# Where a batch's left-over queries stand in the slot order of a fused top-k attention and feed-forward kernel

## The chip, the cores and the metric

The kernel runs as one program on one core of one Trainium2 chip. The metric is the device time of one execution in microseconds; lower is better. Three runs of the kernel before gave 1451.66, 1452.44 and 1452.67 us, so the median is 1452.44 us.

## The reference

Attention with a top-k mask is followed by a two-layer network with a quick-GELU:

```python
# q, k, v: (8, 8, 576, 64); w_in: (512, 2048); w_out: (2048, 512); all float32
scores = (1 / sqrt(64)) * matmul(q, k.transpose(0, 1, 3, 2))        # 576 x 576 for each of 64 heads
kth    = np.partition(scores, -32, axis=-1)[..., -32:-31]            # the 32nd largest of each row
scores = where(scores >= kth, scores, -1e9)
attn   = exp(scores - max); attn = attn / (sum(attn) + 1e-9)
x      = matmul(attn, v).transpose(0, 2, 1, 3).reshape(4608, 512)    # tokens x (head, head_dim)
h      = x @ w_in
out    = (h * sigmoid(1.702 * h)) @ w_out                            # 4608 x 512
```

## The kernel before, in words

**Slots.** Each of the 8 batches has 8 heads, taken as 4 pairs, and 576 queries. 576 is four tiles of 128 queries and 64 left over. A slot is one piece of attention work: 128 query rows for two "heads" of 576 keys. A full slot is one tile of 128 queries for one pair of heads, `(b, t, (hp, hp))`, so there are 16 of them in a batch. The left-over 64 queries of two pairs share one slot, `(b, NF, (hp, hp + 1))`, so there are 2 more; the code calls these `ends`. That makes 18 slots in a batch (`PER`) and 144 in all. The list `slots` (lines 277 to 284) is their order.

**One slot through the engines.** `scores` (line 287) makes the products on TensorE (PE), line 297. `copy_scores` brings them to SBUF on ScalarE (ACT), line 309. `topk_of_pairs` (line 354) finds the 32nd largest on VectorE (DVE) with rounds of MAX8 and MATCH_REPLACE8 (lines 369 and 372); `pair_up` (line 333) makes the larger of each two scores on DVE, line 338, and the smaller on GpSimd (POOL), lines 342 and 352. `mask` and `exps` (lines 426 and 434) run on ACT, `invert` (lines 442 and 444) on DVE, `normalize` (line 457) on POOL. `split` (lines 489 to 495) takes the float32 words apart into halves on ACT and stores them in DRAM; `turn_by_dma` (line 501) brings them back transposed as the tile `pt`. `values_at` (line 560) multiplies `pt` with the values `v_l` and `v_e` on PE, and `x_of` (lines 574 and 577) copies the result into `xT` on ACT.

**Blocks.** `xT` has five places of 128 rows by 512 columns. Place `(b, t)` is complete when the four pairs of tile `t` are done; the ends of an even batch and of the odd batch after it share one place, which is complete when the odd batch's ends are done. `finish_x` then puts a `Block` on the list `ready`. A block is 16 column tiles of the hidden layer. `hidden` (line 605) makes one unit: with one block ready it takes 4 column tiles of this block, 16 matmuls with 128 moving columns; with two blocks ready it takes 2 column tiles of both together, 8 matmuls with 256 moving columns (line 621, many == 2). Either way a unit fills one PSUM bank, and a block is 4 units' worth. `tanh` (lines 643 and 646, ACT), `gate` (lines 655 and 656, POOL) and `project` (line 676, PE, 4 matmuls of 512 columns) take each unit further; `leave` (line 684) brings a finished block out.

**The order of work.** Everything is recorded in one order by hand (`manual_schedule`). Slots 0 to 10 go one by one (`slot`). From slot 11 on, `two_slots(n)` handles slots n and n + 1; it is called a step below. In a step PE gets, in this order: the first `hidden` unit and a `project`, the scores of slot n + 2, the values of slots n - 3 and n - 2 (`held`), the scores of slot n + 3, the second `hidden` unit, and a `project`. When `ready` is empty, `hidden` does nothing. After the last step `last_slot` works off what is left.

**The table of loads.** `later` maps a slot to calls. For batch b and pair hp, relative to the batch's first slot: `FETCH` says when q and k are loaded (q at the number, k one slot later), `READY` when they are split for the transposing load (`prepare_by_dma`, lines 248 to 261), and `VALUES` when `load_v` (lines 200 and 208, three DMAs) runs. All of these DMAs are issued by the queue of SyncE (SP), in program order, between `split`'s store (line 495) and the transposing load (line 501) of the same slot:

```python
        if live(n):
            split(n)
        begin(todo[1])          # loads of v, q and k that stand at slot n + 1
        if live(n):
            turn_by_dma(n)
```

Of the kernel before, what the change touches and what calls it, by code (L numbers as in the profile page):

```python
# [30 lines left out]
def kernel(  # L31
# [32 lines left out]
    NP = H // 2  # L64
# [212 lines left out]
    slots = []  # L277
    for b in range(B):

        full = [(b, t, (hp, hp)) for t in range(NF) for hp in range(NP)]  # L280
        ends = [(b, NF, (hp, hp + 1)) for hp in range(0, NP, 2)]
        slots += full[: -NP] + ends + full[-NP:]
    N = len(slots)
    PER = N // B
    st = [{} for _ in slots]
# [419 lines left out]
    def at(n, fn, *args):  # L705
        later.setdefault(n, []).append((fn, args))
# [1 line left out]

    READY = (-13, -9, -5, -1)
    READY_1 = (-5, -3, -1, 1)
    FETCH = (-17, -15, -11, -7)
    FETCH_1 = (-11, -9, -4, -2)
    VALUES = (0, 1, 2, 3)
    by_slot = dict(enumerate([2, 2, 3, 3, 3, 3, 3, 3, 3, 3, 3, 1]))
    for n in by_slot:
        first = sum(map(len, list(by_slot.values())[:n]))
# [10 lines left out]
    for b in range(1, B):  # L729
        for hp in range(NP):  # L730
            if b > 1:
                for i, name in enumerate("qk"):
                    at(b * PER + FETCH[hp] + i, load, name, b, hp)
                at(b * PER + READY[hp], prepare_by_dma, b, hp)
            else:
                at(b * PER + FETCH_1[hp], load_both, b, hp)
                at(b * PER + READY_1[hp], prepare_by_pe, b, hp)
            at(b * PER + VALUES[hp], load_v, b, hp)
    unfinished = []
    early = []  # L740
    finished = []
# [335 lines left out]
```

## Time and profile before

| What | Value |
|---|---|
| Median of the runs | 1452.44 us (1451.66 to 1452.67) |
| The profiled execution's own time | 1453.04 us |
| Its span in the trace | 1451.2 us |
| PE, PEld busy | 1414.1 us (97%), 995.2 us (69%) |
| DVE busy | 1361.8 us (94%) |
| ACT, POOL busy | 1159.9 us (80%), 985.2 us (68%) |
| Granted TensorE clock | 0.991 |
| DMA bytes moved | 244.40 MB, mean 168 GB/s |

PE is TensorE's matmuls and PEld its weight loads; DVE, ACT, POOL and SP are VectorE, ScalarE, GpSimd and SyncE, and SPq and its like are an engine's own queue, where DMAs are issued. A float32 matmul of the program is two records in the trace, so a unit of 16 matmuls shows as x32 and a unit of 8 as x16. A busy share is an average over stages: which engine sets the pace has to be read stage by stage. The span has three of them: up to about 240 us, where weights are prepared and the first slots run; 240 to 1366 us, where step follows step; and the tail after the last scores at 1366 us.

### The profile page before, as it was taken

To read this page: it belongs to the slowest core of one execution; us is meant where nothing else is said; L and a number is where in the kernel's file an instruction comes from. 1 tells how busy PE (TensorE), PEld (TensorE's weight loads), DVE (VectorE), ACT (ScalarE), POOL (GpSimd) and SP (SyncE) were. 2 spreads that over 40 slices of the span, in tenths; PEclk is the share of its full clock that TensorE was granted. 3 is DMA by queue.
4 is the path that set the end of the run, shared out by engine and by line. 5 is a ranking of instruction groups with operands and counts; after the bars stand their busy time and mean duration, and the time that the engine had idled before them with its cause. 6 is when DMAs were issued, how large, how long until landed. Compare 5 with 4: busy or idle time off the path is not lost.

```text
span 1451.2 us, 29107 instructions
## 1 busy us (share of the span) xinstructions
PE 1414.1 (97%) x9524; PEld 995.2 (69%) x9524; DVE 1361.8 (94%) x4703; ACT 1159.9 (80%) x1862; POOL 985.2 (68%) x1181
## 2 busy tenths in 40 slices
PE   7889899999999999999999999999999999999998
PEld 5667567777666667777666667777666667777665
DVE  7999999999999999999999999999999999999910
ACT  6998887888888887888888888888878888777730
POOL 4888766676766777766667677766777777667610
PEclk8999999999999999999999999999999999999999
DMA  7542467766777768778677767867677776544430
GB/s 212 162 160 63 139 164 195 184 180 171 190 199 186 176 172 209 188 177 189 167 190 185 186 176 185 209 177 186 163 199 192 183 177 179 163 134 129 137 90 15
DMA packets 521272, 244.40 MB, mean 168 GB/s; under 512 B 457376, under 2 KB 495264, under 8 KB 521120
## 3 DMA queue, kind: packets, MB, share of 16 engines
q1 hardware_dynamic: 520688, 242.25, 64.2%
q8 instruction: 75, 1.23, 0.3%
q14 instruction: 77, 0.63, 0.1%
q10 hardware_dynamic: 432, 0.30, 0.1%
HBM read 45.09 MB, written 103.42 MB: 102 GB/s over the span
## 4 chain that ended last, share of the span: by engine, by line
PE 85%; DVE 11%; ACT 1%; DMA 1%; SPq 1%; issue 1%; POOL 0%; DVEq 0%; POOLq 0%
PE ph L621 33%; PE po L676 31%; PE o L560 10%; PE s_ps L297 10%; DVE top L319 3%; DVE left L322 3%; DVE top L369 2%; DVE left L372 1%; DMA pt<-rows 1%; DVE greater L338 0%; ACT sc L493 0%; DVE lesser L372 0%; DVE wout L154 0%; POOL pr L457 0%; DVE win L154 0%
## 5 line engine op out<-in xcount | busy, mean ns | idle before, releaser
L621 PEld LDWEIGHTS ph<-xT,win 128*128 128x128 f32 x3520 | 484.3, 191 | 86.0 <-issue 54.5
L621 PE MATMUL ph<-xT,win 128*128 128x128 f32 (+1 forms) x3520 | 537.4, 309 | 1.0 <-ACT xT L542 0.6
L676 PE MATMUL po<-wout,th 128*128 128x512 f32 x1152 | 519.3, 593 | 4.9 <-POOL wout L149 3.9
L493 ACT COPY sc<-pr 128x2304 uint16<-128x2304 uint16 x134 | 283.1, 2113 | 163.6 <-POOL pr L457 163.6
L676 PEld LDWEIGHTS po<-wout,th 128*128 128x128 f32 x1152 | 213.0, 190 | 217.8 <-issue 205.1
L369 DVE MAX8 top<-left 128x8 f32<-128x288 f32 x810 | 328.0, 446 | 0.0
L342 POOL TENSOR_TENSOR lesser<-sc,greater 128x576 int32<-128x576 int32 x135 | 190.6, 1412 | 177.1 <-DVE greater L338 177.1
L457 POOL TENSOR_SCALAR pr<-pr,rden 128x576 f32<-128x576 f32 x268 | 196.4, 745 | 127.4 <-DVE top L376 76.8
L372 DVE MATCH_REPLACE8 left<-top,left 128x288 f32<-128x288 f32 x540 | 234.8, 442 | 0.0
L434 ACT ACTIVATE pr<-sc,low 128x576 f32<-128x576 f32 x288 | 220.8, 773 | 0.0
L369 DVE MAX8 top<-lesser 128x8 f32<-128x288 f32 x540 | 218.0, 444 | 0.0
L426 ACT ACTIVATE sc<-sc,cut 128x576 f32<-128x576 f32 x288 | 207.4, 774 | 1.8 <-POOL cut L413 1.7
L309 ACT ACTIVATE sc<-s_ps 128x576 f32<-128x576 f32 x288 | 171.0, 648 | 37.1 <-PE s_ps L297 36.2
L352 POOL TENSOR_TENSOR lesser<-lesser,sc 128x576 int32<-128x576 int32 x135 | 190.6, 1412 | 0.2
L297 PE MATMUL s_ps<-qk_t 64*128 64x288 f32 (+1 forms) x1280 | 182.7, 431 | 0.5 <-ACT qk_t L220 0.5
L656 POOL TENSOR_TENSOR th<-th,h 128x512 f32<-128x512 f32 x131 | 167.6, 1279 | 11.2 <-POOL th L655 0.4
L297 PEld LDWEIGHTS s_ps<-qk_t 64*128 64x128 f32 (+1 forms) x1280 | 99.3, 177 | 78.1 <-issue 60.1
L560 PE MATMUL o<-pt,v_l 128*64 128x128 f32 (+1 forms) x2400 | 145.9, 265 | 3.7 <-DMA pt<-rows 3.5
L560 PEld LDWEIGHTS o<-pt,v_l 128*64 128x64 f32 x2400 | 121.4, 137 | 31.3 <-issue 16.9
L338 DVE TENSOR_TENSOR greater<-sc 128x576 f32<-128x576 f32 x135 | 133.2, 986 | 0.0
L655 POOL TENSOR_SCALAR th<-th 128x512 f32<-128x512 f32 x131 | 80.9, 617 | 58.8 <-ACT th L643 58.8
L643 ACT ACTIVATE th<-ph 128x512 f32<-128x512 f32 x144 | 85.5, 594 | 40.1 <-PE ph L621 35.5
(78 smaller groups left out, 1355.5 us busy)
## 6 DMA issues: line engine op xcount, KB each, us to landing
rows<-sc SPq DMA_DIRECT2D x134, 576.0 KB, 3.2
qk_rows<-halves SPq DMA_DIRECT2D x48, 256.0 KB, 2.8
qk_l<-in_q_dram SPq DMA_DIRECT2D x64, 128.0 KB, 3.4
raw<-in_moe_w_in_dram SPq DMA_DIRECT2D x16, 512.0 KB, 4.6
v_l<-in_v_dram SPq DMA_DIRECT2D x32, 256.0 KB, 3.7
raw<-in_moe_w_out_dram SPq DMA_DIRECT2D x16, 512.0 KB, 3.5
out_dram<-ob SPq DMA_DIRECT2D x32, 256.0 KB, 2.9
qk_l<-in_k_dram SPq DMA_DIRECT2D x62, 128.0 KB, 3.4
```

Of the source, the lines that this page charges most:

```text
L297: nc.tensor.matmul(ps[i][rows, c, 0:HALF], lhsT=qT[b, hps[p]][on, cols], rhs=kT[b, hps[p]][on, FIRST[i] + c * HALF : FIRST[i] + (c + 1) * ...
L342: nc.gpsimd.tensor_tensor(out=whole, in0=a.bitcast(I32), in1=greater[n][:].bitcast(I32), op=ALU.subtract)
L352: nc.gpsimd.tensor_tensor(out=whole, in0=whole, in1=b.bitcast(I32), op=ALU.add)
L369: nc.vector.max(found(r, i, True), src[:, i, :])
L372: nc.vector.match_replace(to[:, i, :], found(r, i), src[:, i, :], LOWEST)
L426: nc.scalar.activation(sc[:, i, :], sc[:, i, :], AF.Prelu, bias=cut[:, i : i + 1], alpha=HUGE)
L434: nc.scalar.activation(pr[:, i * S : (i + 1) * S], sc[:, i, :], AF.Exp, bias=low[:, i : i + 1], accum_out=den[:, i : i + 1],)
L457: nc.gpsimd.tensor_scalar(pr[:, i, :], pr[:, i, :], st[n]["rden"][:, i : i + 1], 1.0, op0=ALU.mult, op1=ALU.mult)
L493: nc.scalar.copy(out=halves, in_=pr[:].bitcast(U16).rearrange("p (k h) -> p h k", h=2))
L560: nc.tensor.matmul(o[j * D : (j + 1) * D, cols], lhsT=main[:, j, c, :] if c < NF else tail[:, j, :], rhs=pt[:, MAIN[j] + c if c < NF else ...
L621: nc.tensor.matmul(ph[:, i * many * P : (i + 1) * many * P], lhsT=win[:, c, f * P : (f + 1) * P], rhs=xs[:, first : first + step * (many - ...
L676: nc.tensor.matmul(x.po[:], lhsT=gT[:, i * P : (i + 1) * P], rhs=wout[:, f, :], start=(x.done == 0), stop=(x.done == FC - 1))
```

## The change

In even batches the two `ends` slots move from positions 12 and 13 of the batch to 16 and 17, the last. In odd batches they move to positions 4 and 5, behind the first four full slots. The full slots keep their order among each other. In odd batches the third pair's q and k are split two slots later, and the loads of v stand at slots 2, 2, 3 and 4 of the batch instead of 0, 1, 2 and 3. (`READY` is used from the third batch on; the second batch has `READY_1`, which is not changed.)

```diff
-        slots += full[: -NP] + ends + full[-NP:]
+        first = NP if b % 2 else len(full)
+        slots += full[:first] + ends + full[first:]
...
-    READY = (-13, -9, -5, -1)
+    READY = (-13, -9, -5, -1), (-13, -9, -3, -1)
     READY_1 = (-5, -3, -1, 1)
     FETCH = (-17, -15, -11, -7)
     FETCH_1 = (-11, -9, -4, -2)
-    VALUES = (0, 1, 2, 3)
+    VALUES = (0, 1, 2, 3), (2, 2, 3, 4)
...
-                at(b * PER + READY[hp], prepare_by_dma, b, hp)
+                at(b * PER + READY[b % 2][hp], prepare_by_dma, b, hp)
...
-            at(b * PER + VALUES[hp], load_v, b, hp)
+            at(b * PER + VALUES[b % 2][hp], load_v, b, hp)
```

No instruction on SBUF data is added or removed in attention. What changes with the slot order is when blocks become ready. Before, a batch pair's nine blocks are complete at slots 3, 7, 11, 17, 21, 25, 29, 31 and 35 of its 36; after, at 3, 7, 11, 15, 21, 23, 27, 31 and 35. Of the 144 units of `hidden`, the program before makes 68 with two blocks and 76 with one; the changed program makes 112 with two and 32 with one.

## The prediction

> **What bounds the kernel now.** I read the chain of waits first. It is almost all PE:
>
> ```profile
> PE 85%; DVE 11%; ACT 1%; DMA 1%; SPq 1%; issue 1%; POOL 0%; DVEq 0%; POOLq 0%
> ```
>
> In order of time the DVE part lies before 240 us. From there to 1366 us the chain is PE without a gap, in two kinds of step, one after the other here:
>
> ```profile
> 1200.09 3.65 PE ph L621 x16
> 1203.74 3.43 PE po L676 x8
> 1207.17 3.45 PE ph L621 x16
> 1210.63 3.43 PE po L676 x8
> ...
> 1218.74 3.77 PE ph L621 x32
> 1222.51 3.44 PE po L676 x8
> 1225.94 3.57 PE ph L621 x32
> 1229.51 3.44 PE po L676 x8
> ...
> 1237.62 3.77 PE ph L621 x32
> ```
>
> A step with two-block (wide) units lasts 18.65 us (1200.09 to 1218.74), one with one-block (single) units 18.885 us. From the step whose values start at 258.74 to the one at 1366.17 there are 29 single and 30 wide steps: 29 x 18.885 + 30 x 18.65 = 1107.2, against 1107.4 in the trace.
>
> PE's lead is thin, though. In a wide stage the timeline of DVE shows the line of `pair_up` at a fixed spacing:
>
> ```profile
> 401.92 1.26 DVE L338 TENSOR_TENSOR greater<-sc 128x576 f32<-128x576 f32 x1
> ...
> 411.60 0.73 DVE L338 TENSOR_TENSOR greater<-sc 128x576 f32<-128x576 f32 x1
> ...
> 420.61 1.25 DVE L338 TENSOR_TENSOR greater<-sc 128x576 f32<-128x576 f32 x1
> ```
>
> 9.68 + 9.01 = 18.69 us, in every wide step. DVE has no gap there, so this is its own floor, 0.04 above PE's wide step. In single stages it is held up; the view of line 442 from 250 to 1366 us says by whom:
>
> ```profile
>   ACT pr L434: 3.0, 11
> ```
>
> ACT waits for PE and DVE for ACT, 3.0 us in all. Summed over the L338 spacings, DVE loses 4.2 us to PE over the 117 slots after 251 us. A PE saving beyond that meets DVE.
>
> The third thing is SP's queue. Between a slot's store (L495) and its transposing load (L501) stand the loads of that slot. Slot 2 of a batch is the fullest now (timeline of SP):
>
> ```profile
> 400.02 0.35 SPq L495 DMA_DIRECT2D rows<-sc  x1
> 400.43 0.43 SPq L200 DMA_DIRECT2D v_l<-in_v_dram  x1
> 400.90 1.62 SPq L208 DMA_DIRECT2D v_e<-in_v_dram  x2
> 402.57 1.27 SPq L186 DMA_DIRECT2D qk_l<-in_k_dram  x2
> 403.89 0.63 SPq L189 DMA_DIRECT2D qk_l<-in_k_dram  x1
> 404.63 2.49 SPq L501 DMA_TRANSPOSE pt<-rows  x1
> ```
>
> Load L501 comes 4.6 us after the store; without loads it is 2.85. It lands 4.5 to 4.8 us after its issue here, and the values that need it (second half of L560) start at 410.32, 5.7 after it. So 1.1 us are to spare, in the wide stage, where PE is never idle.
>
> **Part 1, wider units.** The changed program has 44 more wide units in place of single ones: 22 steps x 0.235 us = 5.2 us less on PE. The row behind it is 3.77 against 3.65 and 3.57 against 3.45: 0.12 us for each unit.
>
> The Trainium skill (TensorE: Matmul & The Clock Gate, section "Wait — 56ns, not 53.3ns?") gives a fixed cost of about 2.5 ns for a matmul on a warm array. By it the 16 fewer records of a wide unit would save 0.04 us, 1.8 us in all, where the rows give 0.12 and 5.2. The measured rows decide.
>
> **Part 2, DVE's floor.** DVE's work is the same. 59 steps at 18.69 are 1102.7 us against 1106.9 now, so DVE alone gives back at most 4.2 us.
>
> The Trainium skill (Perfetto Trace Analysis, section "Identifying the Most-Contended Engine") judges TensorE by its weight loads and the other engines by occupancy. That reads 69% against DVE's 94% and makes DVE the bound; the sum by it would be DVE's own waits, 3 to 4 us, not 5.2. The chain's row names PE. Here both are nearly bounds.
>
> **Part 3, the start.** Two `hidden` calls find no block ready. Now they are the second of step 17 and the first of step 19 (203 to 216 us), in the changed order the second of 21 and the first of 23. So PE has 14.3 us more to do just when it is still catching up. I follow it from the scores that end at 207.69: single unit, project, split of q and k, unit, project give the scores of slot 21 at 223.0 (now 216.6); values of ends, scores, unit, project end at 234.8, and `leave` of the third block waits for that on ACT (now 231.8). DVE's L442 waits for the exponentials behind it: about 3.45 us later, at 238.3, now 235.6. So DVE is 2.7 us late; 0.5 of this is the L338 that runs 1.25 instead of 0.74 beside a gate, given back in the step without one. The store that is at 249.64 now comes at 252.35, effectively 251.85 after that 0.5. PE then has a step with little to do and waits; its values start at 259.1 (now 258.74). Bounds: 0 late if ACT had slack there, 4 if the wait recurs; I take 2.2 net, as the L684 row at 231.78 has only 0.3 us of slack to L442.
>
> **Part 4, the loads of v.** In odd batches slot 2 now carries two `load_v` and k of the next batch: nine issues ahead of L501. The extra three cost 0.43 + 1.62 and gaps, 2.1 us. L501 is then issued 4.6 + 2.1 = 6.7 us after its store; plus 4.6 to land, minus 1.15 (the first half of L560 comes first), values may start 10.15 us after the store ("the need"; 6.7 us usually). Now that distance is 9.4 at its largest in a single stage, 8.9 in a wide one. Queued behind L501 on SP is only the next store; waiting for it is PE, and PE is in order, so scores, units and projects wait too. Batches 1, 3 and 5 have this; in batch 1 PE waits for DVE anyway, and in batch 7 there is no next k (need 8.2, covered). Need from both sides: 8.05 if the extra issues hide like today's, 12.5 if an issue is held 1 us (the L189 at 572.03 took 1.59, not 0.63) and the landing takes 6. I take 10.15, since every duration has its row.
>
> **Part 5, the rest at nothing.** The third split moves from step -5 to -3: one ACT copy (L248, 2.1 us), four issues on SP (2.3 us) and one transposing load (3.3 us). Step -3 has no loads in the changed order, ACT is 80% busy, and the keys are needed a step later; uncovered it costs 2.1 us in each of three batches. The other v loads move away from slots 0 and 1 (lighter by 2.1) to slot 4 (k and v, 4.6, need 8.05). Ends cost PE the same in any place, and at least two xT places stay free.
>
> **The sum,** by starts of values. To batch 3: DVE stores at 251.85 + 17 x 18.69 = 569.6; + 10.15 = 579.7, now 577.55. PE alone would be there at 259.1 + 18.89 + 16 x 18.65 = 576.4, so it stalls 3.3 us. To batch 5: 569.6 + 18 x 18.69 = 906.0, plus 1.2 because PE, now late, holds DVE until the distance is back near 9.0; + 10.15 = 917.3, now 915.24; PE alone 915.9. To the last step, 24 steps: 4 x 18.885 + 20 x 18.65 = 448.5 against 450.9: 1365.8 against 1366.17. The tail of 85 us has the same units (8 wide, 2 single). So 0.4 us less than the profiled 1453.04; off the median of 1452.44 that is 1452.0. The end moves by twice the need: 1345.5 + 2 x need.
>
> **Rivals.** A: the need is hidden (under 8.9). Then the slot-4 loads of batch 5 set PE's date: 924.7 + 8.05, and 3 single and 20 wide steps follow: 1362.4, so 1448.6 us. For it: 1.1 us to spare now; against it: the queue is in order and 2.1 exceeds 1.1. B, slower: the nine issues in a row are held up and the landing is late. At a need of 12.2 the end is 1369.9, 1456.1 us; it decides from a need of 11.8. For it: the 1.59 above and landings up to 6.8 in the trace; against it: L501 on the second slot mostly lands in 4.5 to 4.8. C: DVE's floor gives way because POOL's gate no longer overlaps L338 (it does so by 0.64 in every step now), 18.18 a step. Then PE alone counts, 5.1 us less: 1447.3. Against it: the overlap is the same at distances from 8.9 to 9.6.
>
> **How the numbers follow.** Forecast (need 9 to 11.8, 1449.5 to 1455.3): 0.62. A: 0.19. C: 0.05. B: 0.14. No change is within 0.2% (2.9 us), about what a measurement of this kernel tells apart. So faster 0.24, same 0.62, slower 0.14. The range, 1448.4 to 1455.6, takes in A and the start's bounds and leaves out C and most of B.
>
> **What would show it.** Right: x1792 records of L621 with 256 columns; L338 spaced 18.69 across long wide stages; PE waiting for pt<-rows near 578 and 916 us, 1 to 3.5 us each; L501 6.7 us behind its store there. Wrong: no such waits (A), more than 4 us of them (B), L338 spacing under 18.6 (C), or DVE waits of many us elsewhere.

## The result and the profile after

| | Before | After |
|---|---|---|
| Median of the runs | 1452.44 us (1451.66 to 1452.93, 5 runs) | 1457.77 us (1457.22 to 1460.18, 5 runs) |
| Profiled execution, its span | 1453.04, 1451.2 us | 1457.92, 1455.8 us |
| Granted TensorE clock | 0.991 | 0.987 |
| PE, DVE busy | 1414.1, 1361.8 us | 1411.8, 1361.6 us |

The changed kernel is slower: the ratio is 1.0040, with an interval of 1.0025 to 1.0055. The forecast was 1452.0 us and the range ended at 1455.6. Neither engine has more to do; PE even has 2.3 us less. In the changed kernel the helpers' lines stand one further down (L339 for L338, L443 for L442, L496 and L502 for the store and the turning load, L561 for the values, L622 and L677 for the units).

The chain of waits by engine of the kernel after is cut short, since it can be followed back only to 822 us:

```profile
PE 36%; DVE 6%; SPq 0%; DMA 0%; ACT 0%; issue 0%; POOL 0%; ACTq 0%
```

What it covers is PE again. In order of time, the place that was shown of before now has wide units throughout, and a step takes 18.65 us (1206.49 to 1225.14):

```profile
1206.49 3.65 PE ph L622 x16
1210.14 3.43 PE po L677 x8
1213.58 3.45 PE ph L622 x16
1217.03 3.43 PE po L677 x8
...
1225.14 3.65 PE ph L622 x16
```

So this stage is as forecast. The slot that was to decide, the second of batch 3, is as forecast too (timeline of SP; start, duration):

```profile
574.21 0.35 SPq L496 DMA_DIRECT2D rows<-sc  x1
...
576.73 0.59 SPq L200 DMA_DIRECT2D v_l<-in_v_dram  x1
...
578.52 1.27 SPq L186 DMA_DIRECT2D qk_l<-in_k_dram  x2
...
580.56 2.67 SPq L502 DMA_TRANSPOSE pt<-rows  x1
```

The turning load is issued 6.35 us after the store (forecast 6.7) and lands at 585.24, and PE waits for it (timeline of PE; in brackets the idle time and what ended it):

```profile
585.38 1.09 PE L561 MATMUL o<-pt,v_l 128*64 128x128 f32 x16 [1.17 <-DMA pt<-rows]
```

The loss is elsewhere. The best measure of it is the start of each slot's store, which follows DVE, against the same slot's store in before. The table has it for the kernel after and for five of the experiments below, in us behind before (slots count from 0). At slot 10, where the slot orders don't differ yet, the other profiles lie from 0.1 us ahead of before to 0.8 us behind it (fetch_shifted, which has products added ahead of that slot, lies 2.9 behind), so differences of this size say nothing:

| Slot (before at) | after | start_only | batch0_k_earlier | v_late_only | both_mended | all_but_batch0 |
|---|---|---|---|---|---|---|
| 12 (165.4) | 0.66 | -0.07 | -0.17 | -0.12 | 0.04 | 0.37 |
| 13 (175.2) | 2.42 | 1.56 | 1.51 | -0.12 | 1.85 | 0.37 |
| 17 (212.8) | 2.70 | 1.84 | 2.12 | -0.32 | 2.13 | -0.32 |
| 18 (221.1) | 4.62 | 3.76 | 4.03 | -0.32 | 2.13 | -0.32 |
| 20 (239.8) | 5.56 | 5.55 | 5.00 | 0.89 | 2.14 | -0.31 |
| 22 (258.5) | 6.23 | 5.92 | 6.18 | 2.37 | 3.21 | -0.33 |
| 25 (287.1) | 6.73 | 6.04 | 6.17 | 2.82 | 2.17 | -0.31 |
| 55 (568.2) | 6.02 | 5.42 | 6.26 | 3.06 | 2.32 | -0.74 |
| 61 (624.8) | 6.75 | 5.23 | 6.24 | 4.60 | 2.24 | -1.27 |
| 97 (962.5) | 7.35 | 5.23 | 6.24 | 5.44 | 1.92 | -2.37 |
| 143 (1391.7) | 5.01 | 5.23 | 6.24 | 5.44 | -0.21 | -4.37 |

The kernel after is 6.7 us late by slot 25. Behind it the column stays between 6.0 and 7.4 us and ends at 5.0. The windows of the start tell how. First before, then after (columns: window, its length, busy time and instructions of PE, PEld, DVE, ACT and POOL, granted clock, DMA share, GB/s):

```profile
165.00:170.00 5.00, 5.00 (x52) 4.34 (x49) 5.00 (x20) 4.61 (x10) 2.94 (x4) 1.00 0.32 126
200.00:240.00 40.00, 38.11 (x253) 24.50 (x251) 39.66 (x145) 31.93 (x54) 25.62 (x33) 1.00 0.69 173
258.00:264.00 6.00, 6.00 (x71) 4.91 (x68) 6.00 (x22) 5.59 (x12) 3.42 (x4) 1.00 0.68 161
264.00:270.00 6.00, 6.00 (x33) 4.09 (x32) 5.93 (x25) 3.75 (x5) 4.21 (x7) 1.00 1.06 223
```

```profile
165.00:170.00 5.00, 3.31 (x28) 2.55 (x32) 5.00 (x17) 3.19 (x5) 2.96 (x4) 0.67 0.33 128
200.00:240.00 40.00, 40.00 (x341) 29.44 (x341) 37.65 (x133) 32.21 (x58) 26.55 (x33) 1.00 0.58 153
258.00:264.00 6.00, 1.25 (x21) 1.01 (x20) 5.90 (x25) 4.68 (x5) 4.63 (x6) 0.86 0.88 213
264.00:270.00 6.00, 5.56 (x36) 4.22 (x37) 5.93 (x23) 4.03 (x10) 1.68 (x2) 0.57 0.53 183
```

There are three things to see. From 200 to 240 us the roles of PE and DVE are exchanged: PE is busy without a gap and DVE loses 2 us, where before DVE was full and PE had 1.9 us to spare. From 258 to 264 us PE has next to nothing to do. And at 165 and at 264 us the clock falls to 0.67 and 0.57, where before it is 1.00. The two falls go with the two longest waits of PE for a turned block:

```profile
166.69 1.97 PE L561 MATMUL o<-pt,v_l 128*64 128x128 f32 x16 [2.24 <-DMA pt<-rows]
...
264.44 1.97 PE L561 MATMUL o<-pt,v_l 128*64 128x128 f32 x16 [5.19 <-DMA pt<-rows]
```

The same 16 records take 1.09 us after the wait of 1.17 us above, and 1.97 here. The second wait is in the step with little to do. Its block belongs to slot 21, and in the changed order this slot's loads hold a v as well as k, so the turning load is issued 4.57 us after the store (timeline of SP), where before it was 3.30:

```profile
255.19 0.35 SPq L496 DMA_DIRECT2D rows<-sc  x1
...
259.76 2.33 SPq L502 DMA_TRANSPOSE pt<-rows  x1
```

### The profile page after: what moved, and what is told of

It is laid out like the page before. It is cut to its first block, busy times and chain, and to the rows that moved or that the text cites. A ratio compares the mean times of both kernels' runs of the same rounds, so it can differ in the third digit from the quotient of the medians.

```text
span 1455.8 us, 27733 instructions
## 1 busy us (share of the span) xinstructions
PE 1411.8 (97%) x8820; PEld 973.2 (67%) x8820; DVE 1361.6 (94%) x4703; ACT 1159.2 (80%) x1862; POOL 984.7 (68%) x1181
## 5 line engine op out<-in xcount | busy, mean ns | idle before, releaser
L622 PE MATMUL ph<-xT,win 128*128 128x256 f32 (+1 forms) x2816 | 532.3, 344 | 0.5 <-ACT xT L543 0.5
L677 PE MATMUL po<-wout,th 128*128 128x512 f32 x1152 | 519.1, 593 | 4.9 <-POOL wout L149 3.9
L622 PEld LDWEIGHTS ph<-xT,win 128*128 128x128 f32 x2816 | 453.9, 191 | 101.3 <-issue 48.5
L677 PEld LDWEIGHTS po<-wout,th 128*128 128x128 f32 x1152 | 216.4, 190 | 220.5 <-issue 205.1
L561 PE MATMUL o<-pt,v_l 128*64 128x128 f32 (+1 forms) x2400 | 147.8, 267 | 10.3 <-DMA pt<-rows 10.2
L561 PEld LDWEIGHTS o<-pt,v_l 128*64 128x64 f32 x2400 | 122.5, 138 | 38.9 <-issue 25.5
L339 DVE TENSOR_TENSOR greater<-sc 128x576 f32<-128x576 f32 x135 | 133.0, 985 | 1.9 <-ACT sc L310 1.9
```

What stands on the lines that cost most here:

```text
L561: nc.tensor.matmul(o[j * D : (j + 1) * D, cols], lhsT=main[:, j, c, :] if c < NF else tail[:, j, :], rhs=pt[:, MAIN[j] + c if c < NF else ...
L622: nc.tensor.matmul(ph[:, i * many * P : (i + 1) * many * P], lhsT=win[:, c, f * P : (f + 1) * P], rhs=xs[:, first : first + step * (many - ...
L677: nc.tensor.matmul(x.po[:], lhsT=gT[:, i * P : (i + 1) * P], rhs=wout[:, f, :], start=(x.done == 0), stop=(x.done == FC - 1))
```

## The experiments

Each kernel was timed beside the kernel before on the same chip. Ratios are to that kernel, with their intervals; its medians were 1452.4 to 1453.1 us.

### Is it the start?

**from_batch2**: the new order and the late loads of v from batch 2 on only.

```diff
-        first = NP if b % 2 else len(full)
+        first = (NP if b % 2 else len(full)) if b > 1 else len(full) - NP
-            at(b * PER + VALUES[b % 2][hp], load_v, b, hp)
+            at(b * PER + VALUES[b % 2 if b > 1 else 0][hp], load_v, b, hp)
```

> The new slot order and the later loads of v hold from the third batch on; the first two batches are as before. Theory S (the loss is made in the start: PE gets two more units between 200 and 240 us, runs dry afterwards and comes back on a lower clock): the store that the profile of before has at 249.6 us is back there, and with 104 wide units and the two fuller load slots (batches 3 and 5, one wait of up to 1 us and one of 1 to 2 us) the time is about 1450.7 us. Theory L (the loss is made later, by the waits for the values' transposing loads and the new places of the left-over slots): about 1457 us, as the changed kernel's 1457.8.

Measured: 1453.45 us, 1.0002 (0.9993 to 1.0011). The loss is gone, but there is no gain. The time lies between what the two theories gave. Behind the start its PE waits 4.3 us for turned blocks, 1.4 of it behind the nine issues of batch 3 and 2.7 behind those of batch 5, more than in the kernel after (2.5 us).

**start_only**: the other half, batches 0 and 1 changed and the rest as before.

```diff
+        first = (NP if b % 2 else len(full)) if b < 2 else len(full) - NP
+                at(b * PER + READY[0][hp], prepare_by_dma, b, hp)
+            at(b * PER + VALUES[b == 1][hp], load_v, b, hp)
```

> The kernel after with the new places of the left-over slots (and the late loads of v) in batches 0 and 1 alone; the order, the split of q and k and the loads of v of batches 2 to 5 as before. Theory P (the step in which TensorE has few or no units of the output stage moved back from steps 17 to 19, where its slack let TensorE catch up, to steps 21 to 23, where TensorE is late already; five steps of 19.9 us then hold VectorE, which needs 18.7): the start loses by itself what it lost in the kernel after, 4.9 to 6 us, and nothing later gives it back, so about 1458.0 us. Rival R (the start's lag is there only because of what the later order takes away, or is taken back by VectorE's own pace later): 1455.0 or less.

Measured: 1459.04 us, 1.0045 (1.0032 to 1.0057). The start alone loses 6.2 us, and little gives it back: the table's column is 6.0 at slot 25 and 5.2 from slot 61 to the end. Theory P holds in that the start loses this much by itself; R is out.

### Mending one thing in the kernel after

**units_postponed**: the two units that replaced empty calls in steps 17 and 19 are skipped, so they are made later, when PE has little to do.

```diff
-        hidden(ps_t if opens else None)
+        if n != 19:
+            hidden(ps_t if opens else None)
...
-        hidden(ps_t)
+        if n != 17:
+            hidden(ps_t)
```

> The changed kernel with its slot order and loads whole, but the second unit of step 17 and the first of step 19 are left for the two calls of steps 21 and 23 that found no block. So PE has in each step of the start what it has before the change. Theory S: no run-dry wait of 5 us near 260 us, store of slot 21 near 250 us instead of 255.2, time about 1450 us. Rival (the left-over slots at 16, 17, 22 and 23 cost the start by themselves, not the units' dates): 1456 us or more.

Measured: 1458.41 us, 1.0032 (1.0020 to 1.0045). The wait of 5 us near 260 us is gone in its profile, as Theory S had it, and the store of slot 21 is 2.5 us behind before and not 5.6. But PE now waits for the block behind the nine issues of batch 1, and the clock falls there:

```profile
243.60 1.98 PE L561 MATMUL o<-pt,v_l 128*64 128x128 f32 x16 [2.55 <-DMA pt<-rows]
```

From slot 17 to slot 25 its stores fall back by 3.1 us, as in v_late_only below. The profiled execution was the fastest of five, 1455.55 us.

**k_fetched_earlier**: q and k of the first pair of even batches are fetched one slot earlier, so that slot 2 of odd batches issues six loads and not nine.

```diff
-                    at(b * PER + FETCH[hp] + i, load, name, b, hp)
+                    at(b * PER + FETCH[hp] + i - (hp == 0 and b % 2 == 0), load, name, b, hp)
```

> The changed kernel with q and k of an even batch's first pair fetched one slot earlier, so that slot 2 of an odd batch carries six issues between store and transposing load instead of nine. Theory Q (the 6.4 to 6.7 us between store and load are the issues' own time, and they cost twice: the wait of PE, then PE holding DVE back): the load comes 4.7 us after its store in batches 3 and 5, PE's waits of 1.17 and 0.86 us near 585 and 923 us are gone, and the time is about 1453.9 us, 3.9 less than the changed kernel. If the waits are only an echo of the late start: 1457 us.

Measured: 1457.27 us, 1.0026 (1.0014 to 1.0037). The wait at batch 3 is gone in its profile, but the start is as late as in the kernel after: 7.1 us at slot 25.

**kept_warm**: 22 products of the identity in front of the second values of step 23, where PE waits 5.2 us.

```diff
+            if n == 23 and i:
+                idle = ps_t.tile([P, 512], F32, name="idle", tag="tp")
+                for _ in range(22):
+                    nc.tensor.matmul(idle[:, 0:P], lhsT=ident[:], rhs=ident[:], start=True, stop=True)
```

> The changed kernel with 22 products of the identity (128 columns, about 5 us) put into the step without units, ahead of the values that waited 5.19 us for their transposing load. They change no result. Theory S with the lower clock as a part of it: the granted clock from 264 to 270 us goes from 0.57 to about 1.0, the first half of the values there takes 1.1 us instead of 1.97, and the later steps come 1.7 us earlier: about 1456.0 us. If the lower clock is a mere companion of the wait, or DVE alone sets the date: 1457.8 us.

Measured: 1458.08 us, 1.0034 (1.0021 to 1.0046). In its profile the clock from 264 to 270 us is 1.00, and the store of slot 25 is 3.9 us behind before and not 6.7. The added products account for 1.8 us of this: from slot 20 to slot 25 the stores gain 0.6 us, where those of the kernel after fall back by 1.2. The rest lies ahead of the products. The late landing at 165 us came in this execution too, but the clock did not fall behind it (timeline of PE), and slot 13 falls back against slot 12 by 0.2 us, where in the kernel after it is 1.8:

```profile
166.30 1.09 PE L561 MATMUL o<-pt,v_l 128*64 128x128 f32 x16 [2.24 <-DMA pt<-rows]
```

The profiled execution then fell back by 4.1 us between slots 55 and 61, 3.3 more than the kernel after: in batch 3 one of the nine issues was held (SP and PE; the issues of the pair take 1.11 us in the kernel after):

```profile
574.49 2.52 SPq L208 DMA_DIRECT2D v_e<-in_v_dram  x2
```

```profile
584.27 1.98 PE L561 MATMUL o<-pt,v_l 128*64 128x128 f32 x16 [2.92 <-DMA pt<-rows]
```

A wait of 2.92 us there, and the half clock behind it, ate the gain. So none of the three showed the cause: each took away what it was meant to, and the time stayed at 1457 to 1458 us.

### The parts of the start, one by one

**batch0_only**: batch 0's left-over slots last, everything else as before, also the early loads of v. In this kernel the loads of batch 1 are recorded ahead of the last use of v by batch 0, so for two of its pairs the left-over queries of batch 0 meet rows of v of batch 1.

```diff
+        first = len(full) - NP if b else len(full)
```

> Before, with the left-over slots of batch 0 alone put last (20 and 21 in place of 16 and 17). Theory P: tile 4 of batch 0 is then finished two slots earlier and the next tile four slots after that of before, so the step without units stands at 21 to 23; most of the start's loss is here, about 1457 us. Rival V (batch 1's left-over slots at 26 and 27 with its late loads of v make the loss): 1453.5 or less.

Measured: 1469.30 us, 1.0112 (1.0097 to 1.0128), by a cause that neither theory had: SP stands still from the store of slot 17 until a buffer of v is free, 11.6 us (timeline of SP), and the turning load waits behind it.

```profile
214.78 0.34 SPq L496 DMA_DIRECT2D rows<-sc  x1
226.77 0.39 SPq L200 DMA_DIRECT2D v_l<-in_v_dram  x1
```

It shows what the late loads of v are needed for: an order with the left-over slots last keeps all four buffers of v in use into the next batch.

**batch1_only**: batch 1 alone, with its order and its late loads of v.

```diff
+        first = NP if b == 1 else len(full) - NP
+            at(b * PER + VALUES[b == 1][hp], load_v, b, hp)
```

> Before, with batch 1 alone changed: its left-over slots at 26 and 27 and its loads of v late. Theory P: the light step stays at 17 to 19 and the start loses next to nothing; about 1453.5 us (the nine DMA issues of its slot 2 may hold back one turning load, under 1 us). Rival V: 1457 us or more.

Measured: 1455.70 us, 1.0018 (1.0009 to 1.0027), between the two. PE waits 2.76 us at 241.8 us for the block behind the nine issues, and the 16 records behind the wait take 1.98 us.

**batch0_v_late**: batch 0's order, batch 1's loads of v late, batch 1's order as before.

```diff
+        first = len(full) - NP if b else len(full)
+            at(b * PER + VALUES[b == 1][hp], load_v, b, hp)
```

> Before, with batch 0's left-over slots last (16 and 17 in place of 12 and 13) and batch 1's loads of v late, which that order needs; batch 1's own order and all of batches 2 to 7 as before. start_only cost 6.2 us and batch1_only 2.8 us. If the two batches' losses add, 3.4 us are left for batch 0: about 1456.3 us. Rival 1 (the dry step of TensorE, which both orders together make, is the loss): about 1453.5 us. Rival 2 (batch 0's order alone makes the whole loss): about 1459 us.

Measured: 1458.46 us, 1.0040 (1.0027 to 1.0053). With batch1_only's 2.8 us it makes 8.2, and start_only has 6.2. The two are not separate parts, since both have the late loads of v of batch 1 and so the nine issues. The profiled execution was the fastest of five, 1456.95 us.

**v_late_only**: the order of before, only the loads of v late.

```diff
-    VALUES = (0, 1, 2, 3)
+    VALUES = (0, 1, 2, 3), (2, 2, 3, 4)
```

> Before, with nothing but the loads of v of all odd batches late (two of them in slot 2). If the nine DMA issues of that slot are what batch1_only lost by (2.8 us, with one wait of 2.8 us and a low clock behind it), 1455.5 us or more; if they cost only where the order gives them no room, 1453 to 1454 us.

Measured: 1458.99 us, 1.0045 (1.0031 to 1.0058). The loads alone cost 5.9 us. By the table 3.1 us of it come in batch 1 (slots 18 to 25), 1.5 in batch 3 and 0.8 in batch 5. In batch 1 (timeline of PE):

```profile
242.42 1.98 PE L560 MATMUL o<-pt,v_l 128*64 128x128 f32 x16 [2.69 <-DMA pt<-rows]
```

**v_late_k_earlier**: the same, with q and k fetched one slot earlier (the line of k_fetched_earlier).

> v_late_only (the order of before, loads of v of odd batches late), with the first pair's q and k of even batches fetched one slot earlier, so that no slot issues two loads of v and k together (six issues in place of nine). v_late_only lost 5.9 us. Theory N (the nine issues in one slot cost that, in batches 1, 3 and 5): the loss goes, 1453.0 to 1454.0 us, and the granted clock after 240 us is 1.0. Rival (two loads of v in one slot are enough, or v lands too late itself): 1456 us or more.

Measured: 1452.85 us, 1.0001 (0.9992 to 1.0010). The whole loss goes. Two loads of v in one slot cost nothing; k behind them does.

**batch0_k_earlier**: batch0_v_late with q and k fetched one slot earlier, so batch 0's order alone.

> batch0_v_late (batch 0's left-over slots last, batch 1's loads of v late, the rest as before; +5.4 us), with the first pair's q and k of even batches fetched one slot earlier. If the nine issues of batch 1 are over half of its loss and the units' dates (TensorE runs 19.9 us a step while VectorE needs 18.7) are the rest, about 1455.5 us, near what the prediction gave the start (2.2 us late). Rival (the units' dates and the dry step behind them make all of it, and the nine issues are hidden since TensorE is late): 1458 us or more.

Measured: 1459.34 us, 1.0044 (1.0031 to 1.0057). The loss stays whole, so batch 0's order makes 6.6 us by itself, without any slot of nine issues. Its windows are those of the kernel after:

```profile
200.00:240.00 40.00, 40.00 (x333) 29.57 (x332) 37.47 (x132) 32.20 (x58) 26.44 (x32) 1.00 0.63 161
...
258.00:264.00 6.00, 0.24 (x6) 0.00 (x0) 5.90 (x24) 4.68 (x5) 4.07 (x6) 0.77 0.87 191
264.00:270.00 6.00, 5.76 (x41) 4.74 (x42) 5.93 (x23) 4.42 (x10) 2.24 (x3) 0.66 0.60 191
```

**both_mended**: the kernel after with units_postponed and k_fetched_earlier at once.

> The kernel after with both changes at once that alone brought next to nothing: the second unit of step 17 and the first of step 19 skipped (units_postponed), and q and k of even batches' first pair one slot earlier (k_fetched_earlier). Theory T (two causes cover one another: when TensorE is late with units the nine issues are hidden, and when it is not they are on the path): about 1454 us. Rival (a third cause holds the start, such as the landing that falls on a fetch of code, or the step that has too little to do): 1457 us or more.

Measured: 1452.13 us, 0.9995 (0.9986 to 1.0004). Two edits that alone brought nothing that these runs can tell bring 5.6 us together (1457.77 to 1452.13). The nine issues alone lose 5.9 us (v_late_only), batch 0's order alone 6.6 (batch0_k_earlier), both together no more, and only with both mended is the time back at that of before. The start isn't whole even then: in this profile the store of slot 25 is still 2.2 us late, 1.8 of it from the landing at 165 us, and the part behind it gives 2.4 back. With the units at their late date PE is busy when the block behind the nine issues is due, so that wait is hidden; with the units out of the way PE waits there instead, 2.55 us at 243.6 us in the profile of units_postponed.

### The late landing at 165 us

In the profile of the kernel after the turned block of slot 11 lands 6.0 us after its issue, in that of before after 4.7. The DMA queues in that window of the kernel after have one packet that before's have not:

```profile
q8 instruction: 1, 0.02, 1.2%
```

It is a fetch of 16 KB of code at 164.4 us; in before the nearest is at 154.7. The same split runs through the other kernels: with batch 0's new order the fetch is at 163.6 to 164.4 us in all ten but fetch_shifted, and in eight of these nine the block takes 6.0 to 6.3 us (in batch0_v_late 4.6); with the old order the fetch is at 154.5 to 155.7 us in all eight, and it takes 4.5 to 4.7.

**fetch_shifted**: 32 more warming products in slot 2, so that PE's stream of instructions is shifted.

```diff
-            stay_warm(8)
+            stay_warm(40 if n == 2 else 8)
```

> The kernel after, with 32 more products of the kind that keeps TensorE warm, in slot 2, where TensorE waits 3.2 us anyway: TensorE's instruction stream is shifted by some 64 instructions, a quarter of a fetched block, and so are all later fetches of its code. Theory F (the turned block of slot 11 lands 6.0 us after its issue and not 4.6 because a 16 KB fetch of instructions at 164.4 us lies in it; in before the fetch lies at 154.7 us): it lands after 4.6 us, TensorE's wait of 2.2 us falls to 0.8, the granted clock in 165 to 170 us is 1.0, the store of slot 13 comes 1.4 to 1.8 us earlier, and the time is about 1456.3 us unless another landing is hit. Rival (the late landing has another cause): 6.0 us again and 1457.8 us.

Measured: 1459.33 us, 1.0042 (1.0029 to 1.0054), so no gain in time. The steps of Theory F came all the same: the fetches now stand at 141.9 and 170.1 us, and the block lands after 4.8 us (DMA issues from 160 to 169 us):

```profile
pt<-rows SPq DMA_TRANSPOSE x1, 4.8
```

PE waits 1.0 us there, the clock from 165 to 170 us is 1.00, and the store of slot 13 no longer falls back against that of slot 12 (2.37 and 2.38 us behind before, where the kernel after goes from 0.66 to 2.42). But the added products had already made slot 10 2.9 us late, so the time can't show the gain.

The late landing costs by the clock that falls behind it. In kept_warm and units_postponed the block is as late and PE waits 2.24 us for it, but the clock stays at 1.00, and slot 13 falls back against slot 12 by 0.2 us only, not by 1.8.

### What the later part is worth

**q_k_shifted**: from_batch2, with q and k of batches 4 and 6 fetched one slot earlier.

> The kernel from_batch2 (new order and late loads of v from batch 2 on, the start as before), with the first pair's q and k of even batches from 4 on fetched one slot earlier, so that the slot with two loads of v in batches 3 and 5 no longer issues k too. In from_batch2's profile VectorE's lead over before fell by 0.5 us net at the heavy slots of batch 3 and by 1.9 us net at those of batch 5 (waits of TensorE for the turned block of 1.4 and 2.7 us). Theory H (that issue costs from_batch2 its gain): about 1451.0 us. Rival (the waits are an echo, and something else is late next): 1453.4 us.

Measured: 1449.48 us, 0.9977 (0.9968 to 0.9985). Theory H holds: the nine issues took from_batch2's gain.

**single_units**: the same with `blocks = ready[:1]`, so that no unit is wide.

> q_k_shifted (1449.5 us) with the hidden units always one block wide (the first of the ready blocks alone), which takes away what the order is for. By the rows, a pair of units of one block takes 0.12 us more than the wide one of two, 104 of them 12.5 us of TensorE. Theory W (the wide units are where the gain comes from, and TensorE sets the pace once they are gone): 1455 to 1462 us. Rival (VectorE's 18.7 us a step covers it): 1449.5 to 1451 us.

Measured: 1460.46 us, 1.0050 (1.0038 to 1.0063), 11.0 us more than q_k_shifted, where the rows gave 12.5. The wide units are where the gain comes from: by 0.11 us for each, the 36 that q_k_shifted has more than before make 3.8 us, and it gained 3.4.

**all_but_batch0**: q_k_shifted with the new order in batch 1 too, and batch 1's loads of v early.

```diff
-        first = (NP if b % 2 else len(full)) if b > 1 else len(full) - NP
+        first = (NP if b % 2 else len(full)) if b > 0 else len(full) - NP
```

> q_k_shifted (order of before in batches 0 and 1, new order from batch 2 on, late loads of v in batches 3, 5 and 7, q and k of the first pair of batches 4 and 6 one slot earlier; 1449.5 us) with the new order in batch 1 too, its loads of v as before, since batch 0's left-over slots are not last. It has as many wide units as the kernel after (112 against 104). If batch 0's order alone is what the start loses by, this keeps all that the change can bring: 8 more wide units less 0.12 us each, about 1448.5 us. Rival (batch 1's order by itself also holds VectorE, as batch 0's does): 1451 us or more.

Measured: 1447.92 us (1447.27 to 1448.30), 0.9968 (0.9956 to 0.9980). This beats both kernels. It has the 112 wide units of the kernel after, and its start looks like that of before:

```profile
200.00:240.00 40.00, 37.66 (x268) 24.01 (x266) 39.66 (x145) 31.91 (x53) 25.66 (x34) 1.00 0.71 176
...
258.00:264.00 6.00, 6.00 (x72) 4.96 (x69) 5.99 (x21) 5.48 (x12) 3.08 (x3) 1.00 0.55 164
```

## Why the prediction was wrong

**The failed step is Part 3, the start.** It put DVE 2.7 us late, 2.2 net and at most 4, and priced nothing but the two units; the start lost 6.7. It said that two units move from steps 21 and 23 into 17 and 19, that PE is late then, that the store of slot 21 comes 2.7 us late, and that a step with little to do follows. That store came at 255.19 us, 5.6 late. The units' own share is what was worked out: the stores of slots 18 and 20 fall back by 1.9 and 0.9 us, and the scores of slot 21 start at 225.58 us, 2.6 later than the 223.0 of the sum, which is the lateness that slot 17 had already. The rest was missing:

- The landing of slot 11's block on a fetch of code, and the low clock behind that wait: 1.8 us between the stores of slots 12 and 13. Nothing in the trace of before showed it, since there the fetch falls elsewhere; whether the clock falls behind it is chance, and it did in six of the eight profiles with this late landing. With 0.7 us that were there at slot 10 and 0.3 behind slot 13 it makes the 2.7 us of slot 17.
- The step with little to do. The prediction let PE wait and start its values at 259.1 us as before. In the trace the second half of these values starts at 264.44 us, because the store they need is late itself, and from 264 to 270 us PE has a mean clock of 0.57. From slot 20 to slot 25 the stores fall back by another 1.2 us. One size was wrong too: 259.1 is the store's 252.35 plus the usual need of 6.7, but this slot loads v and k, for which the prediction's own Part 5 has 8.05. The trace has 264.44 - 255.19 - 1.15 = 8.1.
- The bound "4 if the wait recurs", which was the upper end for the start. The loss of 6.7 us is 2.7 beyond it, more than the 2.2 us by which the median lies beyond the range.

**One clause of Part 4 failed too**: "in batch 1 PE waits for DVE anyway". v_late_only loses 3.1 us there. In the changed kernel PE waits only 0.27 us for that block, but only because it is late with the units; so the clause cost the forecast nothing, and would have cost any plan to mend the start.

**The other steps held.** Part 4's need, 10.15 us, was 9.9 in batch 3 (585.24 - 574.21 - 1.15) and 10.1 in batch 5 (923.57 - 912.34 - 1.15). PE waited 1.2 and 0.9 us there, less than the 3.3 and 1.4 worked out: at batch 3 the store was 4.6 us later than in the sum (574.21 against 569.6), but PE 6.5 (its values start at 582.90, against 576.4), so most of the stall had no room. Part 1's 0.12 us for each unit is confirmed by single_units: 11.0 us for 104 wide units is 0.11. Part 2's floor of 18.69 us shows in the spacing of L339: from 287 us to the end, 52 of 58 steps lie between 18.67 and 18.70 us, and before it was 41 of 58 from 280 us on. From slot 25 on the sum is off by 0.9 us: it gave back 2.6 (from 2.2 late to 0.4 early), and the trace gives back 1.7 (6.73 to 5.01).

**The rivals.** A's mechanism, a hidden need, is not in the kernel after. It can be had by moving k: q_k_shifted's 1449.5 and all_but_batch0's 1447.9 us stand where A put the time, 1448.6. B asked for a need over 11.8, which did not come in the timed kernel's profile; the loss came from another place, so B's time, 1456.1 us, is near by luck. One execution, the profiled one of kept_warm, shows B's mechanism by itself: an issue held for 1.4 us and 4.1 us lost. C did not happen: no step is shorter than 18.67 us.

**What stays open.** No run takes batch 0's 6.6 us apart cleanly. The profiles give a rough split. From slot 12 to slot 25 the stores fall back by 6.1 to 7.1 us in after, start_only, batch0_k_earlier and k_fetched_earlier, where the clock fell at 165 us. In batch0_v_late and fetch_shifted, where the block landed in time, it is 3.3 and 3.7 us. So about 3 us go with the landing and its low clock, and the rest with the units and the step with little to do. Each of these is a single execution, and the two without the low clock at 165 us are the fastest of their kernels' five, so the split of the medians may be another. What the v in slot 21's loads costs by itself was not tried.

## What to carry to other kernels

Where two engines are within a per cent of each other, an order that moves work of one of them by a few steps is priced by what the other one waits for in just those steps, not by the sum of work: draw the start step by step, as carefully as the steady stage. When mending one suspect brings nothing, don't drop it; take away two at once, because a late engine hides a late transfer and the other way round. And keep the queue of a dependent load short: three more issues behind two loads in one slot, in three batches, cost 5.9 us here, and all that the order could bring was 4.5.

## What the runs showed of the hardware

**The clock falls after short waits.** Over all profiles after 160 us, PE waited 40 times for 0.7 to 1.7 us in front of a first product of values, and the 16 records behind it took 1.1 us or less each time. Of 14 waits of 2.2 to 2.9 us nine were followed by 1.95 to 1.98 us for the 16 records and one by 1.67; of eight waits of 4.3 us and more all were (1.72 to 1.98). The Trainium skill (TensorE: Matmul & The Clock Gate, section "HAM oscillation — how this bites in real kernels") says that gaps of over about 3.4 us are to be avoided. Here 2.2 us were enough more often than not.

What decides can be read from the traces' clock records. In them the clock is at half for 3.4 us or a multiple of it, and within one execution all these stretches start on one grid of 3.41 us: in the kernel after at 153.07, 166.72 and 262.29 us, which are 4 and 28 steps apart. In the kernel after the wait from 164.45 to 166.69 us lies between two borders of this grid, and the clock fell at the second. In kept_warm, whose grid has a border at 164.44 us, the wait from 164.06 to 166.30 us lies across it, 1.86 us of it behind the border, and the clock stayed. So it goes for all 62 waits: the clock fell with each of the 19 that have 1.96 us or more between two borders, and with none of the 43 that have at most 1.86. The grid lies elsewhere in each execution, so it is chance whether a wait of 2.2 to 2.7 us brings the low clock. The same page (section "Part 1: The HAM clock gate") has the window running freely, which agrees with this.

**A turning load with a fetch of code in its flight often lands late.** Of the 158 transposing loads in the profile of before, 52 have a 16 KB fetch of PE's instructions (queue q8) in their flight, and 19 of these land after more than 5.9 us; of the other 106 one does. In the kernel after it is 14 of 45 and none of 113. The Trainium skill (Runtime: NRT & Kernel Launch, section "Instruction fetch mechanics") has the instructions fetched in blocks of 16 KiB or 256 instructions, mostly hidden. The size agrees with the packets here, and there are about 250 records of PE and its weight loads from one to the next. But the load of slot 11 landed 6.0 us after its issue with the fetch in its flight and after 4.8 when fetch_shifted had moved it. That run shows that an edit which changes the number of instructions on PE, even far ahead, can move such a delay off one load, and then perhaps onto another.
